# A gated attention and MLP kernel: K, V and Q products of chunks 2 to 8 written as pairs of 64-row halves

## The chip, the cores and the metric

The kernel runs on one NeuronCore of one Trainium2 chip. The metric is the time of one execution on the device, in microseconds (us). Five engines work beside each other, each through its own instruction queue: TensorE (PE for its matmuls, PEld for the weight loads that go with them), VectorE (DVE), ScalarE (ACT), GpSimd (POOL) and SyncE (SP), which here only issues DMAs.

## The reference

Two branches read the same x (2048 tokens of 512 features) and are mixed by a gate per token:

```
qkv = x @ wqkv                                   # 32 heads of 16
pq, pk = q @ w_phi[h], k @ w_phi[h]
phi(p) = concat(softmax(p), softmax(-p))         # per head, 16 + 16 features
kv = sum_s phi_k[s]^T v[s];  z = sum_s phi_k[s]
a  = (phi_q kv / (phi_q z + 1e-6)) @ wo
b  = mish(x @ w1 + b1) @ w2                      # 512 -> 1376 -> 512
g  = sigmoid(sum(x * gate_w))
out = g * a + (1 - g) * b
```

## The kernel before, in words

All large products are taken in fp32r, with each operand split into a high part (h) and the rest (l); a product of two operands is three: h by h, h by l, l by h.

**Stage A** goes over the 2048 tokens in 8 chunks of 256, key ("A", c) with c from 0 to 7; the text counts them as chunks 1 to 8. `w_phi` is multiplied into the K and Q weights first (`fuse`). For each chunk the 512 x features lie as four groups of 128 on the partitions, in two tiles xh and two tiles xl. A chunk has two token tiles of 128, t = 0 and 1. For each of K, V and Q and each tile, `proj` (L230) sends 3 x 4 = 12 products of 128 contraction rows into one PSUM bank (128 tokens x 512 columns): 72 products in a chunk, 6 banks. The steps k0, k1, v0, v1, q0, q1 stand for these groups of 12. All matmuls go through the helper at L101.

What follows K: VectorE takes the maximum and the minimum of each head (mx, mn, L256), the differences (d0, d1, L270 and L272) into a tile E, ACT the exponential, VectorE the sums S (L276), the reciprocal (L284) and the scaled E (ml, L287). GpSimd adds E to zacc (z, L330). V is copied out of PSUM by ACT (ve), Q too (qe), and Q is then stored to DRAM (st). After chunks 3, 6 and 8 TensorE does the `kv` steps of the chunks since the last time: kvp, small products of E and v in 32-column tiles of the array, 32 per chunk, each two records in the profile. In chunks 7 and 8 VectorE also has work of stage B: the softmax of Q's first tiles (out<-pq), the low parts xbl of stage B's x (XL0, XL1, L431) and the sum of zacc.

**Stage B** goes over 4 blocks of 512 tokens. `up` (12 products each, from xbh, w1 and xbl), Mish on ACT, `down` (12 products for four token tiles), `num` (phi_q by kv, in tiles of 64 rows by 32 columns of the array), `wo`. `cd` is four products of 32 contraction rows at four row places, into the four banks of `down`. In the first `up` the products with xbl come last, and they read both halves of it.

**The order** is written out by hand. Strings such as MID, NEXT and LAST (L42 to L58) list the steps; `run` (L201) calls them in turn, and every instruction is pinned, so each engine has its instructions in the order of the string. In stage A the strings put k0 first, then k1, v0, v1, q0, q1, between the steps of other engines. NEXT is chunk 7, LAST chunk 8. Waits between engines are put in from the tiles that they share.

PSUM has eight banks in three rings: "a" with 3, "dn" with 4, "kv" with 1. K and Q go to "a", V of chunks 2 to 8 to "dn".

Of the kernel before, what the change touches and what calls it, by code (L numbers as in the profile page):

```python
# [14 lines left out]
P = 128  # L15
# [4 lines left out]
KT = D // P  # L20
# [19 lines left out]
    S0 rS0 ml0 z0 ldw0 ldw1 S1 rS1 ml1 z1 q0 qe0 st0 q1 qe1 st1  # L40
"""
MID = """  # L42
    k0 xh mx0 mn0 d00 d10 xl ldx k1 wh0 E0 wl0 ldw0 mx1 mn1 d01 d11 v0 wh1 E1 S0 rS0 ml0 z0 ve0 v1 wl1 ldw1
    S1 rS1 ml1 z1 ve1 q0 qe0 st0 q1 qe1 st1
"""
THREE = MID + """ kv" kv' kv """
SIXTH = """
    k0 xh mx0 mn0 d00 d10 xl ldx k1 wh0 E0 wl0 ldw0 mx1 mn1 d01 d11 v0 wh1 E1 S0 rS0 ml0 z0 ve0 v1 wl1 ldw1 lq0+
    S1 rS1 ml1 z1 ve1 q0 qe0 st0 q1 qe1 st1 mx0+ mn0+ kv" kv' kv
"""  # L50
NEXT = """
    lq1+ d00+ d10+ k0 xh mx0 mn0 d00 d10 xl ldx k1 wh0 E0 wl0 ldw0 E0+ mx1 mn1 d01 d11 wh1 E1 S0 rS0 ml0 z0 v0 ve0 wl1 ldw1
    S1 rS1 ml1 z1 v1 ve1 q0 mx1+ mn1+ d01+ d11+ qe0 st0 q1 qe1 st1 E1+
"""
LAST = """
    lq2+ k0 mx0 mn0 d00 d10 k1 ldw0 E0 XH0 mx1 mn1 d01 d11 wx E1 v0 S0 rS0 ml0 z0 ve0 XH1 S1 rS1 ml1 z1 XL0
    v1 ve1 mx2+ mn2+ XL1 q0 qe0 st0 q1 qe1 st1 zt zf zs S0+ zl kv' kv rS0+ km
"""  # L58


# [29 lines left out]
def tile_gated_mix(ctx: ExitStack, tc: tile.TileContext, xT, wv, wkT, wqT, bd, w1a, w1b, b1, w2a, w2b, wo, out):  # L90
    nc = tc.nc
# [5 lines left out]
    pin = tc.keep_in_program_order  # L97
    V, G_, A_, Sy = nc.vector, nc.gpsimd, nc.scalar, nc.sync

    def mm(*a, **k):  # L100
        return pin(nc.tensor.matmul(*a, **k))  # L101

    def T(shape, dt, tag, bufs, name):
        nm[0] += 1
        return sp.tile(shape, dt, name=f"{name}_{nm[0]}", tag=tag, bufs=bufs)

    def k8(name, tag, dt=F32R):
        return T([P, 2048], dt, tag, 2 if tag in ("eT", "E") else 1, name)
# [4 lines left out]
    def k2(name, tag, dt=F32):  # L113
        return T([P, 512], dt, tag, {"pq": 3, "io": 4, "hl": 8}[tag], name)

    def psum(name, tag, bufs={"a": 3, "dn": 4, "kv": 1}):
        nm[0] += 1
        return pp.tile([P, 512], F32, name=f"{name}_{nm[0]}", tag=tag, bufs=bufs[tag])

    def act(out_, in_, fn=AF.Copy, **k):  # L120
        return pin(A_.activation(out_, in_, fn, **k))  # L121

    def kt(t, f):
        return t[:, : KT * f].rearrange("p (k f) -> p k f", f=f)
# [71 lines left out]
    steps = {}  # L196

    def at(key, name, fn):
        steps.setdefault((key, name), []).append(fn)

    def run(text, key, prev=None, nxt=None, prev2=None):  # L201
        for w in text.split():
            k = {"'": prev, '"': prev2, "+": nxt}.get(w[-1], key)
            for fn in steps.pop((k, w.rstrip("'+\"")), ()):
                fn()


    wkh, wkl, wvh, wvl, wqh, wql = [
        kt(k8(n, t), 512) for n, t in (("wkh", "xbh"), ("wkl", "xbl"), ("wvh", "woh"), ("wvl", "wol"), ("wqh", "eT"), ("wql", "eT"))]
    xs, Es, vs, psA, Ep = {}, {}, {}, {}, {}  # L210
# [19 lines left out]
    def proj(x, t, wh, wl, tag, lo_last=False):  # L230
        ps = psum("proj", tag)
        xh, xl = x
        sl = slice(t * P, (t + 1) * P)
        n = 0
        for a, w in ((xh, wh), (xl, wh), (xh, wl)) if lo_last else ((xh, wh), (xh, wl), (xl, wh)):
            for k in range(KT):
                mm(ps, a[k // 2][:, k % 2, sl], w[:, k, :], start=(n == 0), stop=(n == 3 * KT - 1))
                n += 1
        return ps

    def new_x(c):
        xs[c] = [[k2(n, "hl", F32R)[:, :].rearrange("p (k f) -> p k f", f=SC) for _ in range(2)] for n in ("xh", "xl")]
# [7 lines left out]
    def feat_ops(key, t, src, d):  # L250

        n = str(t)

        def red(name, op):
            d[name] = T([P, H], F32, name, 2, name)
            pin(V.tensor_reduce(d[name], hv(src()), axis=AX.X, op=op))  # L256

        def dd(a):
            if "E" not in d:
                pair = key, t // 2  # L260
                if key == ("A", NCH - 1):
                    d["E"] = k4("E", "oh")
                else:
                    if pair not in Ep:
                        e = T([P, NFB * 512], F32, "w2b", 2, "E")[:, :2048] if key in THIRD else k8("E", "E", F32)[:, :]
                        Ep[pair] = e.rearrange("p (t x) -> p t x", t=2)
                    d["E"] = Ep[pair][:, t % 2, :]
            E = hv(d["E"][:, a * 512 : (a + 1) * 512])
            if a == 0:
                pin(V.tensor_sub(E, hv(src()), d["mx"][:, :, None].to_broadcast([P, H, DH])))  # L270
            else:
                pin(V.tensor_sub(E, d["mn"][:, :, None].to_broadcast([P, H, DH]), hv(src())))  # L272

        def ss():
            d["S"] = T([P, 2 * H], F32, "Sm", 2, "Sm")
            pin(V.tensor_reduce(d["S"], hv(d["E"][:, :]), axis=AX.X, op=ALU.add))  # L276

        at(key, "mx" + n, lambda: red("mx", ALU.max))
        at(key, "mn" + n, lambda: red("mn", ALU.min))
        at(key, "d0" + n, lambda: dd(0))  # L280
        at(key, "d1" + n, lambda: dd(1))
        at(key, "E" + n, lambda: act(d["E"], d["E"], AF.Exp))
        at(key, "S" + n, ss)
        at(key, "rS" + n, lambda: pin(V.reciprocal(d["S"], d["S"])))  # L284
# [4 lines left out]
    def a_ops(c):  # L289
        key = ("A", c)  # L290
        P_ = psA[c] = {}
        for t in range(2):
            d = {}
            Es[c, t] = d

            def k_(t=t):
                P_["k", t] = proj(xs[c], t, wkh, wkl, "a")

            def v_(t=t):
                P_["v", t] = proj(xs[c], t, wvh, wvl, "dn" if c else ("kv", "a")[t], lo_last=not c)  # L300

            def q_(t=t):
                P_["q", t] = proj(xs[c], t, wqh, wql, "a")

            def ve(t=t):
                if key in THIRD:
                    if t == 0:
                        Ep[key, "v"] = T([P, NFB * 512], F32, "w2b", 2, "v")
                    vs[c, t] = Ep[key, "v"][:, t * 512 : (t + 1) * 512]
                else:  # L310
                    vs[c, t] = k2("v", "io")
                act(vs[c, t], P_["v", t])

            def qe(t=t):
                P_["qs", t] = k2("qs", "pq")
                act(P_["qs", t], P_["q", t])

            def st(t=t):
                i = 2 * c + t
                pin(Sy.dma_start(pqd[i * P : (i + 1) * P, :], P_["qs", t]))  # L320

            at(key, f"k{t}", k_)
            at(key, f"v{t}", v_)
            at(key, f"q{t}", q_)
            at(key, f"ve{t}", ve)
            at(key, f"qe{t}", qe)
            at(key, f"st{t}", st)
            feat_ops(key, t, lambda t=t: P_["k", t][:, :], d)
            at(key, f"ml{t}", lambda d=d: scale_by(d, V))
            at(key, f"z{t}", lambda d=d: pin(G_.tensor_add(zacc, zacc, d["E"])))  # L330

        def kv():
            if not kvs:
                kvs.append(psum("kvp", "kv")[:, : NG * 64].rearrange("p (g f) -> p g f", g=NG))
            (kvp,) = kvs
            for t in range(2):
                E, v = Es[c, t]["E"], vs[c, t]
                Ev = E[:, :].rearrange("p (a r b x) -> p b r a x", a=2, r=2, b=8)
                for u in range(8):
                    for r in range(2):  # L340
                        o = (u % 2) * 64 + 32 * r
                        mm(kvp[o : o + 32, u // 2, :], v[:, u * 64 + 32 * r : u * 64 + 32 * r + 32], Ev[:, u, r, :, :],
                           start=(c == 0 and t == 0 and u < 2), stop=(c == NCH - 1 and t == 1), skip_group_check=True)

        at(key, "kv", kv)
        if c + 1 < NCH:
            def xh():
                new_x(c + 1)
                for j in range(2):
                    x_hi(c + 1, j)  # L350

            at(key, "xh", xh)
            for j in range(2):
                at(key, "xl", lambda j=j: x_lo(c + 1, j, G_))
        if c + 2 < NCH:
            at(key, "ldx", lambda: ldx(c + 2))
# [455 lines left out]
    for i in range(4):  # L812
        wh, wl = [halves(w, slice(i // 2 * 2, i // 2 * 2 + 2))[i % 2] for w in (wqh, wql)]
# [6 lines left out]

    for t in range(2):
        psA[0]["k", t] = pk[t]
        del steps[("A", 0), f"k{t}"]

    run(FIRST, ("A", 0))
    for c in range(1, NCH):
# [1 line left out]
        run(text, ("A", c), ("A", c - 1), ("B", 0), ("A", c - 2))  # L828
    for b in range(NB):
        run((BLOCK0, BLOCK1, BLOCK, BLOCK)[b], ("B", b), ("B", b - 1), ("B", b + 1))  # L830
    assert not steps, list(steps)


# [58 lines left out]
```

## Time and profile before

| | us |
|---|---|
| median of 3 runs | 444.58 (444.49 to 446.23) |
| span of the profiled execution | 442.5 |
| stage A, from fuse's end to the last kvp's end | 18.7 to 149.35 |
| stage B | 149.35 to 442.5 |

For the profiled execution the page gives its span, from the first to the last instruction, and no other time. Busy times on the page are by engine; the tenths show the busy share of each of 40 equal slices. The chain that ended last is followed back from the last instruction to what released it. In rows of instructions, `E<-E,Sm` is the tile written and the tiles read, L287 the line, `x48` a count, and a last bracket the engine's idle time just before, with what ended it. Matmuls are pipelined, so that a row's length is longer than the distance from one start to the next, and the ends of matmuls are modelled. The whole-array product of 512 columns is shown with 0.39 us and one starts every 0.227 us. The granted TensorE clock is 0.999 of full speed.

### The profile page before, as it was taken

To read this page: it belongs to the slowest core of one execution; us is meant where nothing else is said; L and a number is where in the kernel's file an instruction comes from. 1 tells how busy PE (TensorE), PEld (TensorE's weight loads), DVE (VectorE), ACT (ScalarE), POOL (GpSimd) and SP (SyncE) were. 2 spreads that over 40 slices of the span, in tenths; PEclk is the share of its full clock that TensorE was granted. 3 is DMA by queue.
4 is the path that set the end of the run, shared out by engine and by line. 5 is a ranking of instruction groups with operands and counts; after the bars stand their busy time and mean duration, and the time that the engine had idled before them with its cause. 6 is when DMAs were issued, how large, how long until landed. Compare 5 with 4: busy or idle time off the path is not lost.

```text
span 442.5 us, 7179 instructions
## 1 busy us (share of the span) xinstructions
PE 437.8 (99%) x2874; PEld 359.9 (81%) x2874; DVE 313.2 (71%) x420; ACT 201.4 (46%) x286; POOL 159.6 (36%) x100
## 2 busy tenths in 40 slices
PE   8999999999999999999999999999999999999996
PEld 7888888888888888887888878888878888887885
DVE  3987739559699999999999898279679329601103
ACT  3644523533345455736376533646352645341330
POOL 3078694785662453621024120215310222411121
PEclk9999999999999999999999999999999999999999
DMA  7721631524403136425362533222605302310002
GB/s 265 283 96 48 191 120 50 188 86 133 167 29 116 49 84 209 142 101 168 128 205 96 159 124 120 75 96 95 191 0 192 94 2 96 134 57 1 0 0 96
DMA packets 29001, 49.64 MB, mean 112 GB/s; under 512 B 6308, under 2 KB 15012, under 8 KB 28968
## 3 DMA queue, kind: packets, MB, share of 16 engines
q1 hardware_dynamic: 28648, 48.79, 32.9%
q8 instruction: 22, 0.36, 0.3%
q10 hardware_dynamic: 288, 0.39, 0.3%
q14 instruction: 11, 0.09, 0.1%
q0 software_dynamic: 32, 0.01, 0.0%
HBM read 31.73 MB, written 16.79 MB: 110 GB/s over the span
## 4 chain that ended last, share of the span: by engine, by line
PE 98%; DMA 1%; SPq 0%; DVE 0%; issue 0%
PE proj L101 30%; PE up L101 27%; PE down L101 27%; PE wo L101 10%; PE kvp L101 2%; PE num L101 2%; DMA wT<-in_wkT_dram 1%; PE fuse L101 1%; PE rest L101 0%; DVE io L709 0%; SPq L157 0%; SPq L149 0%
## 5 line engine op out<-in xcount | busy, mean ns | idle before, releaser
L543 POOL TENSOR_TENSOR l<-act,h 128x512 fp32r<-128x512 f32 (+1 forms) x44 | 62.6, 1425 | 215.5 <-ACT h L121 192.7
L121 ACT ACTIVATE act<-up,b1s 128x512 f32<-128x512 f32 x44 | 30.3, 688 | 83.1 <-PE up L101 81.0
L330 POOL TENSOR_TENSOR zacc<-zacc,E 128x1024 f32<-128x1024 f32 x16 | 39.7, 2479 | 39.9 <-DVE E L287 31.4
L121 ACT ACTIVATE E<-E 128x1024 f32<-128x1024 f32 x32 | 33.5, 1060 | 36.0 <-DVE E L272 35.9
L287 DVE TENSOR_TENSOR E<-E,Sm 128x1024 f32<-128x1024 f32 x32 | 45.1, 1409 | 1.0
L101 PE MATMUL wo<-woh,ohl 128*128 128x512 f32 x128 | 41.2, 389 | 0.0
L276 DVE TENSOR_REDUCE Sm<-E 128x64 f32<-128x1024 f32 x32 | 38.5, 1204 | 0.0
L101 PE MATMUL down<-w2ah,h 128*128 128x512 f32 x96 | 37.6, 392 | 0.0
L101 PE MATMUL down<-w2al,h 128*128 128x512 f32 x80 | 31.2, 390 | 0.0
L101 PE MATMUL down<-w2ah,l 128*128 128x512 f32 x80 | 31.1, 389 | 0.0
L121 ACT ACTIVATE h<-act 128x512 fp32r<-128x512 f32 (+2 forms) x48 | 30.3, 632 | 1.6
L101 PE MATMUL down<-w2bh,h 128*128 128x512 f32 x78 | 30.6, 392 | 0.0
L101 PE MATMUL down<-w2bl,h 128*128 128x512 f32 x78 | 30.4, 389 | 0.0
L101 PE MATMUL down<-w2bh,l 128*128 128x512 f32 x78 | 30.4, 389 | 0.0
L431 DVE TENSOR_TENSOR xbl<-xraw,xbh 128x1024 fp32r<-128x1024 f32 x8 | 10.9, 1378 | 27.1 <-ACT xbh L121 27.1
L256 DVE TENSOR_REDUCE mx<-proj 128x32 f32<-128x512 f32 x16 | 11.0, 689 | 25.5 <-PE proj L101 25.5
L101 PEld LDWEIGHTS wo<-woh,ohl 128*128 128x128 f32 x128 | 24.0, 188 | 5.0
L121 ACT ACTIVATE io<-wo,g_sb 128x512 f32<-128x512 f32 x16 | 11.0, 690 | 36.0 <-PE wo L101 34.7
L121 ACT ACT_TABLE_LOAD x19 | 24.4, 1283 | 3.5 <-PE up L101 3.2
L101 PE MATMUL up<-xbh,w1ah 128*128 128x512 f32 x96 | 25.8, 390 | 0.0
L101 PE MATMUL up<-xbh,w1al 128*128 128x512 f32 x96 | 25.7, 389 | 0.0
L101 PE MATMUL up<-xbl,w1ah 128*128 128x512 f32 x96 | 25.7, 389 | 0.0
(125 smaller groups left out, 978.3 us busy)
## 6 DMA issues: line engine op xcount, KB each, us to landing
ed<-E SPq DMA_DIRECT2D x16, 512.0 KB, 2.9
eT<-ed SPq DMA_DIRECT2D x64, 128.0 KB, 3.2
xraw<-in_xT_dram SPq DMA_DIRECT2D x15, 512.0 KB, 4.3
pqd<-qs SPq DMA_DIRECT2D x16, 256.0 KB, 2.1
pq<-pqd SPq DMA_DIRECT2D x16, 256.0 KB, 3.8
out_dram<-io SPq DMA_DIRECT2D x15, 256.0 KB, 2.0
raw<-in_w1a_dram SPq DMA_DIRECT2D x3, 512.0 KB, 4.6
raw<-in_w2a_dram SPq DMA_DIRECT2D x3, 512.0 KB, 3.7
```

Of the source, the lines that this page charges most:

```text
L101: return pin(nc.tensor.matmul(*a, **k))
L121: return pin(A_.activation(out_, in_, fn, **k))
L256: pin(V.tensor_reduce(d[name], hv(src()), axis=AX.X, op=op))
L276: pin(V.tensor_reduce(d["S"], hv(d["E"][:, :]), axis=AX.X, op=ALU.add))
L287: pin(eng.tensor_mul(hv(d["E"][:, :]), hv(d["E"][:, :]), d["S"][:, :, None].to_broadcast([P, 2 * H, DH])))
L330: at(key, f"z{t}", lambda d=d: pin(G_.tensor_add(zacc, zacc, d["E"])))
L431: pin(V.tensor_sub(xb[b][1][:, :, sl], kt(raw[h], SC), f32(xb[b][0][:, :, sl])))
L543: pin(G_.tensor_sub(U[i]["l"][:n, :], U[i]["a"][:n, :], f32(U[i]["h"][:n, :])))
```

## The change

For chunks 2 to 8 the three groups k0, k1 and v0 are sent as one step `(k0|k1|v0)` at the start of the chunk, and v1, q0 and q1 as another, `(v1|q0|q1)`. In each step the 36 products are listed in order and each is written as two products of 64 contraction rows, rows 0 to 63 and rows 64 to 127. The first row half goes through the list from its start, the second from its middle, and they take turns; so at each turn the two halves write to different banks. K stays in the ring "a"; Q of these chunks moves from "a" to "dn". Chunk 1 keeps whole products.

A bank is first written by one half and later by the other. Where the half changes in a bank, the product waits until the last one of the other half in that bank has ended (`hold`). Of a group's 72 half products four have this wait, 56 in all, each for a product 13 to 15 half products before it.

```diff
+    def weave(ops):
+        n = len(ops)
+        todo = [(r, ops[(i + r * (n // 2)) % n]) for i in range(n) for r in (0, 1)]
+        banks = [op[0].name for _, op in todo]
+        last = {b: i for i, b in enumerate(banks)}
+        for i, (r, (out_, a, w, opens, closes)) in enumerate(todo):
+            b, s = banks[i], slice(64 * r, 64 * r + 64)
+            row, ins = newest.get(b, (r, None))
+            if row != r:
+                hold = pin(nc.tensor.nop())
+                tc.add_manual_dep(hold.ins, ins, ...)
+            ins = mm(out_, a[s], w[s], start=opens and banks.index(b) == i, stop=closes and last[b] == i, skip_group_check=True)
+            newest[b] = r, ins.ins.name
...
+    def proj_ops(ps, x, t, wh, wl):
+        xh, xl = x
+        sl = slice(t * P, (t + 1) * P)
+        return [(ps, a[k // 2][:, k % 2, sl], w[:, k, :], True, True) for a, w in ((xh, wh), (xh, wl), (xl, wh)) for k in range(KT)]
...
+            def one(n, wh, wl, tag, t=t):
+                P_[n, t] = psum("proj", tag)
+                return proj_ops(P_[n, t], xs[c], t, wh, wl)
+
+            if c:
+                for n, wh, wl, tag in (("k", wkh, wkl, "a"), ("v", wvh, wvl, "dn"), ("q", wqh, wql, "dn")):
+                    ops[key, f"{n}{t}"] = lambda n=n, wh=wh, wl=wl, tag=tag, one=one: one(n, wh, wl, tag)
...
 MID = """
-    k0 xh mx0 mn0 d00 d10 xl ldx k1 wh0 E0 wl0 ldw0 mx1 mn1 d01 d11 v0 wh1 E1 S0 rS0 ml0 z0 ve0 v1 wl1 ldw1
-    S1 rS1 ml1 z1 ve1 q0 qe0 st0 q1 qe1 st1
+    (k0|k1|v0) xh mx0 mn0 d00 d10 xl ldx wh0 E0 wl0 ldw0 mx1 mn1 d01 d11 wh1 E1 S0 rS0 ml0 z0 ve0 (v1|q0|q1) wl1 ldw1
+    S1 rS1 ml1 z1 ve1 qe0 st0 qe1 st1
 """
```

The strings SIXTH, NEXT and LAST are changed in the same way. `(k0|k1|v0)` stands where k0 stood, and `(v1|q0|q1)` after ve0. The steps of the other engines keep their order.

More of the change, by code (lines that the diff above doesn't have):

```diff
@@ L47 @@
 SIXTH = """
-    k0 xh mx0 mn0 d00 d10 xl ldx k1 wh0 E0 wl0 ldw0 mx1 mn1 d01 d11 v0 wh1 E1 S0 rS0 ml0 z0 ve0 v1 wl1 ldw1 lq0+
-    S1 rS1 ml1 z1 ve1 q0 qe0 st0 q1 qe1 st1 mx0+ mn0+ kv" kv' kv
+    (k0|k1|v0) xh mx0 mn0 d00 d10 xl ldx wh0 E0 wl0 ldw0 mx1 mn1 d01 d11 wh1 E1 S0 rS0 ml0 z0 ve0 (v1|q0|q1) wl1 ldw1 lq0+
+    S1 rS1 ml1 z1 ve1 qe0 st0 qe1 st1 mx0+ mn0+ kv" kv' kv
 """
 NEXT = """
-    lq1+ d00+ d10+ k0 xh mx0 mn0 d00 d10 xl ldx k1 wh0 E0 wl0 ldw0 E0+ mx1 mn1 d01 d11 wh1 E1 S0 rS0 ml0 z0 v0 ve0 wl1 ldw1
-    S1 rS1 ml1 z1 v1 ve1 q0 mx1+ mn1+ d01+ d11+ qe0 st0 q1 qe1 st1 E1+
+    lq1+ d00+ d10+ (k0|k1|v0) xh mx0 mn0 d00 d10 xl ldx wh0 E0 wl0 ldw0 E0+ mx1 mn1 d01 d11 wh1 E1 S0 rS0 ml0 z0 ve0 (v1|q0|q1) wl1 ldw1
+    S1 rS1 ml1 z1 ve1 mx1+ mn1+ d01+ d11+ qe0 st0 qe1 st1 E1+
 """
 LAST = """
-    lq2+ k0 mx0 mn0 d00 d10 k1 ldw0 E0 XH0 mx1 mn1 d01 d11 wx E1 v0 S0 rS0 ml0 z0 ve0 XH1 S1 rS1 ml1 z1 XL0
-    v1 ve1 mx2+ mn2+ XL1 q0 qe0 st0 q1 qe1 st1 zt zf zs S0+ zl kv' kv rS0+ km
+    lq2+ (k0|k1|v0) mx0 mn0 d00 d10 ldw0 E0 XH0 mx1 mn1 d01 d11 wx E1 S0 rS0 ml0 z0 ve0 (v1|q0|q1) XH1 S1 rS1 ml1 z1 XL0
+    ve1 mx2+ mn2+ XL1 qe0 st0 qe1 st1 zt zf zs S0+ zl kv' kv rS0+ km
 """
@@ L101, in mm @@
         return pin(nc.tensor.matmul(*a, **k))
+    def weave(ops):
[8 more added lines that the diff above has]
+                hold = pin(nc.tensor.nop())
+                tc.add_manual_dep(hold.ins, ins, mybir.DependencyInfo(mybir.DependencyClass.Sync, mybir.DependencyReason.DATA), reason="row tiles take turns in a bank")
+            ins = mm(out_, a[s], w[s], start=opens and banks.index(b) == i, stop=closes and last[b] == i, skip_group_check=True)
+            newest[b] = r, ins.ins.name
+    newest = {}
     def T(shape, dt, tag, bufs, name):
@@ L199, in at @@
         steps.setdefault((key, name), []).append(fn)
+    ops = {}
     def run(text, key, prev=None, nxt=None, prev2=None):
         for w in text.split():
+            if w[0] == "(":
+                weave(sum([ops.pop((key, x))() for x in w[1:-1].split("|")], []))
+                continue
             k = {"'": prev, '"': prev2, "+": nxt}.get(w[-1], key)
@@ L294, in a_ops @@
             Es[c, t] = d
-            def k_(t=t):
-                P_["k", t] = proj(xs[c], t, wkh, wkl, "a")
             def v_(t=t):
-                P_["v", t] = proj(xs[c], t, wvh, wvl, "dn" if c else ("kv", "a")[t], lo_last=not c)
+                P_["v", t] = proj(xs[c], t, wvh, wvl, ("kv", "a")[t], lo_last=True)
             def q_(t=t):
@@ L320, in st @@
                 pin(Sy.dma_start(pqd[i * P : (i + 1) * P, :], P_["qs", t]))
-            at(key, f"k{t}", k_)
-            at(key, f"v{t}", v_)
-            at(key, f"q{t}", q_)
+            def one(n, wh, wl, tag, t=t):
[4 more added lines that the diff above has]
+                    ops[key, f"{n}{t}"] = lambda n=n, wh=wh, wl=wl, tag=tag, one=one: one(n, wh, wl, tag)
+            else:
+                at(key, f"v{t}", v_)
+                at(key, f"q{t}", q_)
             at(key, f"ve{t}", ve)
@@ L822, in tile_gated_mix @@
         psA[0]["k", t] = pk[t]
-        del steps[("A", 0), f"k{t}"]
     run(FIRST, ("A", 0))
@@ L830, in tile_gated_mix @@
         run((BLOCK0, BLOCK1, BLOCK, BLOCK)[b], ("B", b), ("B", b - 1), ("B", b + 1))
-    assert not steps, list(steps)
+    assert not steps and not ops, (list(steps), list(ops))
 _OUTS = [((S, D), 'float32')]
```

## The prediction, made before the changed kernel ran

> **What bounds the kernel now.** I read the page first: the busy times, the busy tenths of VectorE (40 slices of 11.06 us each), the chain by line.
>
> ```profile
> PE 437.8 (99%) x2874; PEld 359.9 (81%) x2874; DVE 313.2 (71%) x420; ACT 201.4 (46%) x286; POOL 159.6 (36%) x100
> ...
> DVE  3987739559699999999999898279679329601103
> ...
> PE proj L101 30%; PE up L101 27%; PE down L101 27%; PE wo L101 10%; PE kvp L101 2%; PE num L101 2%; DMA wT<-in_wkT_dram 1%; PE fuse L101 1%; PE rest L101 0%; DVE io L709 0%; SPq L157 0%; SPq L149 0%
> ```
>
> TensorE sets the end: 98% of the chain is its matmuls. VectorE is nearly full too, from slice 10 (110 us), the end of the projections, to about 240 us. The chain in order of time (start, length, what) gives the pace.
>
> ```profile
> 18.72 41.03 PE proj L101 x180
> ...
> 62.56 49.18 PE proj L101 x216
> 111.75 2.82 PE kvp L101 x192
> 114.56 32.86 PE proj L101 x144
> 147.43 1.92 PE kvp L101 x128
> 149.35 11.10 PE up L101 x48
> ...
> 164.99 2.72 PE up L101 x12
> ...
> 437.75 1.44 PE rest L101 x12
> ```
>
> A product of 512 columns takes 2.72/12 = 0.2267 us, one of 256 columns ("rest") 1.44/12 = 0.120. The 256 columns between them cost 0.1067, so 512 columns stream in 0.2133 and each product has a fixed **gap of 0.0133 us**. Re-entering the projections from kvp's quarter-column products costs once 32.86 - 144 x 0.2267 = 0.22. Chunks 7 and 8 are those at 114.56; each chunk has 72 products, 16.32 us. Next, the stretches by engine (PE, PEld, DVE, ACT, POOL busy): an ordinary chunk, chunks 7 and 8, and what follows.
>
> ```profile
> 62.56:78.90 16.34, 16.34 (x73) 13.55 (x73) 11.45 (x14) 4.33 (x6) 9.92 (x7) 1.00 0.30 95
> ...
> 114.56:131.00 16.44, 16.44 (x74) 13.61 (x74) 13.81 (x18) 6.64 (x8) 9.35 (x5) 1.00 0.25 91
> 131.00:147.40 16.40, 16.40 (x77) 13.32 (x78) 16.26 (x17) 7.24 (x9) 6.67 (x4) 1.00 0.29 97
> 147.40:208.00 60.60, 60.60 (x445) 49.63 (x444) 58.46 (x78) 34.65 (x47) 23.93 (x15) 1.00 0.42 133
> ```
>
> An ordinary chunk leaves VectorE 4.9 us idle; chunk 8 leaves 0.1 and the next 60 us leave 2. So a lateness of VectorE that begins in chunk 7 has nothing to be made up in.
>
> **The change, part by part.**
>
> *Concurrency.* 504 whole products become 1008 half ones. Do two halves run at once? The trace has row tiles already: cd, four 32-row products into four banks, and num, 64-row by 32-column ones.
>
> ```profile
> 205.17 0.39 PE L101 MATMUL down<-w2bl,h 128*128 128x512 f32 x1
> 205.40 0.39 PE L101 MATMUL down<-w2bh,l 128*128 128x512 f32 x1
> 205.72 0.51 PE L101 MATMUL down<-w2al,hc 32*128 32x512 f32 x4
> 206.16 0.44 PE L101 MATMUL num<-eT,kvb 64*32 64x256 f32 x7
> ```
>
> The four cd products, each of 128 output columns and 512 streamed ones like the change's, start at 205.72 and num follows at 206.16: 0.44 us for four with their weight loads and two changes of tile shape, where four whole ones take 0.91. They ran together, loads too. I take two halves to run at once.
>
> *Pace of a pair.* Each half still streams 512 columns, so a pair cannot beat 0.2133, and if each half keeps its own gap the pair takes 0.2267 as one product does now. What is the gap? Weight loads (PEld) beside the matmuls:
>
> ```profile
> 256.27 0.39 PE L101 MATMUL down<-w2ah,h 128*128 128x512 f32 x1
> 256.50 0.39 PE L101 MATMUL down<-w2al,h 128*128 128x512 f32 x1
> ```
>
> ```profile
> 256.27 0.19 PEld L101 LDWEIGHTS down<-w2al,h 128*128 128x128 f32 x1
> 256.50 0.19 PEld L101 LDWEIGHTS down<-w2ah,l 128*128 128x128 f32 x1
> ```
>
> The load for the next product starts as the current one starts and is over 0.04 us before the next one begins. So loading is hidden already and two row halves have no exposed load to hide; the gap belongs to the product itself. Bounds: 0.2133 (the other half covers it) and 0.2400 (it is paid for each half in turn). I take 0.2267, nearest to the whole-array row: no gain and no loss on TensorE itself. The Trainium skill, page "TensorE: Matmul & The Clock Gate", section "The mechanism" of Part 3, says a weight load overlaps running matmuls only when the row groups differ; by it the gap would be exposed loading and the halves would remove it. The two rows above, a load wholly beside a matmul of the same rows, speak against it here.
>
> *Entering the 64-row shape.* Once more than before, between chunks 1 and 2: 0.2 by the 0.22 above; the kvp entries remain. The second half starting just behind the first is under 0.01 per group.
>
> *The holds.* Four products per group of 36 wait for the other half's last product in their bank: 56 waits, the awaited one 13 halves (1.5 us) back. Queued behind each is all of TensorE. A wait of TensorE on itself is in the trace already: in the built order the first product of chunk 1's second Q tile has one, at 24.23.
>
> ```profile
> 23.32 1.07 PE L101 MATMUL proj<-wqh,xl 128*128 128x512 f32 x4
> 24.23 1.07 PE L101 MATMUL proj<-wqh,xh 128*128 128x512 f32 x4
> ```
>
> 24.23 - 23.32 = 4 x 0.2267: it cost nothing. I take 0; the upper end is an emptied array each time, 0.39 - 0.23 = 0.16, 9 us in all.
>
> *Q now in the four-buffer ring, V and Q evictions in a burst.* ACT is idle over half of each chunk above, which hides it; SP's stores stand where they stood, the last one's product ends when it did. The x low parts are needed at the third pair instead of the ninth; POOL makes them a chunk ahead.
>
> *When the products finish.* This is what costs. K tile 0 was done after 12 products; woven, its last half is the 60th of 72: it starts 29 x 0.2267 = 6.58 us into the chunk instead of 11 x 0.2267 = 2.49, so **+4.09**. K tile 1 ends with the group: 35 x 0.2267 = 7.94 instead of 5.21, +2.73. VectorE's softmax starts on these tiles (start, length, [idle before]):
>
> ```profile
> 108.11 1.90 DVE L287 TENSOR_TENSOR E<-E,Sm 128x1024 f32<-128x1024 f32 x1
> ...
> 117.55 0.69 DVE L256 TENSOR_REDUCE mx<-proj 128x32 f32<-128x512 f32 x1 [2.25 <-PE proj L101]
> 118.15 0.68 DVE L256 TENSOR_REDUCE mn<-proj 128x32 f32<-128x512 f32 x1
> ...
> 120.27 0.69 DVE L256 TENSOR_REDUCE mx<-proj 128x32 f32<-128x512 f32 x1 [0.24 <-PE proj L101]
> ...
> 132.11 2.88 DVE L272 TENSOR_TENSOR E<-mn,pq 128x512 f32<-128x512 f32 x1
> 134.91 0.68 DVE L256 TENSOR_REDUCE mx<-proj 128x32 f32<-128x512 f32 x1
> ...
> 144.50 1.90 DVE L287 TENSOR_TENSOR E<-E,Sm 128x1024 f32<-128x1024 f32 x1
> ...
> 148.65 2.21 DVE L431 TENSOR_TENSOR xbl<-xraw,xbh 128x1024 fp32r<-128x1024 f32 x1
> ```
>
> In chunks 2 to 6 the 4.9 us of idle time take the lateness. kvp after chunk 6 needs the scaled E of 108.11, done at 110.0, then 114.0; TensorE reaches that E in the last sixth of kvp, 111.75 + 0.2 + 2.35 = 114.3: just in time.
>
> Chunk 7: the first mx moves from 117.55 by 4.09 + 0.2 to 121.84. Four operations at 0.60 follow, so the second mx stands at 124.25 (its tile is there at 123.2): **+4.0** against 120.27. From 120.27 on no idle time is shown before any operation, so all moves by 4.0; chunk 8's first mx would be at 138.9, its tile there by 138.3, so nothing further is added. Then TensorE meets it twice. Chunk 8's kvp needs E of 144.50 + 1.90 = 146.4, then 150.4, and stands there at 147.43 + 0.2 + 1.44 = 149.1: 1.3 us of stall. And up's third part needs the second xbl, 148.65 + 2.21 = 150.86, then 154.86:
>
> ```profile
> 151.22 1.07 PE L101 MATMUL up<-xbl,w1ah 128*128 128x512 f32 x4
> ```
>
> It started at 151.22, 0.36 later; k0's last product of chunk 7 gives the hand-over (116.44 + 3 x 0.227 + 0.39 = 117.51, mx at 117.55: 0.04).
>
> ```profile
> 116.44 1.07 PE L101 MATMUL proj<-wkh,xl 128*128 128x512 f32 x4
> ```
>
> So 0.32 us of slack: TensorE is put back 4.0 - 0.32 = **3.7 us**, the kvp stall within it. After that TensorE has no gap to make it up, and VectorE, late by as much, keeps its place against it.
>
> Sum: 442.5 (span) + 3.7 = 446.2; the runs' median lies 444.58 - 442.5 = 2.1 above the span (start and end around it, since the page gives no other time of this execution), so **448.3 us**.
>
> **The rivals.**
>
> *The gap is hidden by the other half (not slower).* Pair 0.2133. Chunk 7 starts 5 x 72 x 0.0133 - 0.2 = 4.6 earlier, but K tile 0 comes 29 x 0.2133 - 2.49 = 3.7 later in it: first mx -0.9, second -0.9 + 2.42 - 2.72 = -1.2. VectorE then sets the pace to xbl, and TensorE gains 1.2 + 0.3 = 1.5: 443.1. It decides when two starts in one half stand less than 0.226 apart. For it: the bound is not excluded by any row, as no row has two successive 64x128 products. Against: above. The rule of the Trainium skill quoted above is this rival.
>
> *The gap, or the holds, cost time on TensorE.* Pair 0.2400: chunk 7 starts 4.8 + 0.2 = 5.0 later, K tile 0 comes 29 x 0.24 - 2.49 = 4.5 later, mx +9.5, second +9.2, TensorE +8.9: 453.5. Holds at 0.16: 40 of them before chunk 7, 6.4 us, and with the main case's lateness 455.
>
> *The halves do not run at once.* 504 x 0.2267 = 114 us more, VectorE hidden: 559. The cd rows speak against it.
>
> *VectorE makes it up.* E of 132.11 took 2.88 beside POOL's work where others take 0.68; were such meetings with POOL to fall otherwise, up to 3 us return and the time is about 445.5. Against: the POOL work that it meets
>
> ```profile
> 131.59 2.85 POOL L330 TENSOR_TENSOR zacc<-zacc,E 128x1024 f32<-128x1024 f32 x1
> ```
>
> follows VectorE's own scaled E, and moves with it.
>
> **How the numbers follow.** Main case 0.62 (448.3, its own range 446.3 to 449.5); hidden gap 0.14; VectorE makes it up 0.06; gap or holds paid 0.13; one after the other 0.04; rest 0.01. Faster or slower counts beyond 0.5% (2.2 us), about what a measurement of this kernel tells from no change: 442.4 and 446.8. The hidden gap at its full bound stays inside, but 0.04 may pass it; inside are 0.10 of it, most of the fourth rival and some of the main case: 0.18. Slower 0.78. The range goes from 443.6, most of the hidden gap, to 454.
>
> **What would show it.** Products of one half 0.227 apart, two halves' starts close together (right); 0.213 or 0.24 (rivals); halves in turn at 0.113 each are the same pace. The first mx of chunk 7 about 4.3 us later within a chunk of the old length, VectorE without idle time behind it, TensorE idle about 1.3 us in kvp and 2.2 us before up's xbl. I am wrong if stage A's chunks change length, or if VectorE is late and TensorE does not wait there.

## The result, and the profile after

| | before | changed |
|---|---|---|
| median, us | 444.53 (444.28 to 446.23, 4 runs) | 448.66 (448.51 to 448.71, 4 runs) |
| span of the profiled execution, us | 442.5 | 446.9 |

The changed kernel is slower: its runs to those of before have the ratio 1.0088 (95% interval 1.007 to 1.0106). The forecast was 448.3 us.

The page of the changed kernel, the lines that answer to those of before: engines' busy time, VectorE's tenths, and the chain that ended last.

```profile
PE 439.3 (98%) x3378; PEld 360.5 (81%) x3378; DVE 313.8 (70%) x420; ACT 200.5 (45%) x286; POOL 159.8 (36%) x100
...
DVE  3968556577799999999999998359769329601103
...
PE 64%; DVE 3%; issue 0%
```

The matmul records grow by 504 and TensorE's busy time by 1.5 us: half products in pairs take the time of whole ones. VectorE's busy time is nearly the same. What is new stands in the chain: it was 98% TensorE, and now, followed back from the end, it leaves TensorE at up's xbl and runs through VectorE's work of chunk 8, where the profile traces it no further back (so the shares sum to 67%). The view of waits, of TensorE alone, says where (who waited for whom: us in total, times, longest):

```profile
PE up L101 <- DVE xbl L462: 1.7, 1, 1.7
PE kvp L101 <- DVE E L314: 1.4, 1, 1.4
PE warm L101 <- DVE ones L188: 1.1, 1, 1.1
```

The same view of the kernel before:

```profile
PE warm L101 <- DVE ones L171: 1.1, 1, 1.1
PE fuse L101 <- DMA wT<-in_wkT_dram: 0.2, 1, 0.2
```

The waits in up and kvp are new; the third was there before. Now TensorE in order of time, from chunk 1's last whole products on (start, length, what):

```profile
26.60 1.07 PE L101 MATMUL proj<-wqh,xl 128*128 128x512 f32 x4
27.60 0.49 PE L101 MATMUL proj<-wkh,xh 64*128 64x512 f32 x1
27.60 0.49 PE L101 MATMUL proj<-wkl,xh 64*128 64x512 f32 x1
27.93 0.39 PE L101 MATMUL proj<-wkh,xh 64*128 64x512 f32 x1
27.94 0.39 PE L101 MATMUL proj<-wkl,xh 64*128 64x512 f32 x1
...
35.91 0.39 PE L101 MATMUL proj<-wvh,xh 64*128 64x512 f32 x1
35.92 0.39 PE L101 MATMUL proj<-wql,xh 64*128 64x512 f32 x1
...
42.71 0.39 PE L101 MATMUL proj<-wql,xh 64*128 64x512 f32 x1
42.72 0.39 PE L101 MATMUL proj<-wqh,xh 64*128 64x512 f32 x1
...
44.07 0.39 PE L101 MATMUL proj<-wkh,xh 64*128 64x512 f32 x1
44.08 0.39 PE L101 MATMUL proj<-wkl,xh 64*128 64x512 f32 x1
```

The two halves start within 0.01 us of each other, and the six pairs from 42.71 to 44.07 take 1.36/6 = 0.227 us each, the pace of one whole product before. The whole group (v1|q0|q1) of chunk 2, from 35.91 to the next group's start at 44.07, takes 8.16 = 36 x 0.2267. VectorE from the end of chunk 6's share on (a last bracket is its idle time just before, with the releaser):

```profile
112.69 1.91 DVE L314 TENSOR_TENSOR E<-E,Sm 128x1024 f32<-128x1024 f32 x1
...
117.63 1.78 DVE L299 TENSOR_TENSOR E<-mn,pq 128x512 f32<-128x512 f32 x1
122.47 0.69 DVE L283 TENSOR_REDUCE mx<-proj 128x32 f32<-128x512 f32 x1 [3.05 <-PE proj L101]
...
124.86 0.69 DVE L283 TENSOR_REDUCE mx<-proj 128x32 f32<-128x512 f32 x1
...
139.50 0.68 DVE L283 TENSOR_REDUCE mx<-proj 128x32 f32<-128x512 f32 x1
...
149.09 1.89 DVE L314 TENSOR_TENSOR E<-E,Sm 128x1024 f32<-128x1024 f32 x1
...
153.22 2.22 DVE L462 TENSOR_TENSOR xbl<-xraw,xbh 128x1024 fp32r<-128x1024 f32 x1
```

VectorE sits idle for 3.05 us in front of chunk 7's first maximum, and its timeline shows no idle time again up to xbl. And TensorE there:

```profile
148.19 1.55 PE L101 MATMUL kvp<-E,v 128*32 128x64 f32 x96
151.12 0.65 PE L101 MATMUL kvp<-E,v 128*32 128x64 f32 x32 [1.38 <-DVE E L314]
151.70 1.20 PE L101 MATMUL up<-xbh,w1ah 128*128 128x512 f32 x4
152.74 1.08 PE L101 MATMUL up<-xbh,w1al 128*128 128x512 f32 x4
155.49 1.21 PE L101 MATMUL up<-xbl,w1ah 128*128 128x512 f32 x4 [1.68 <-DVE xbl L462]
```

The last quarter of kvp starts at 151.12, when the E of 149.09 + 1.89 = 150.98 is there; the products with xbl start at 155.49, 0.05 after xbl's 153.22 + 2.22 = 155.44.

### The profile page after: what moved, and what is told of

Its sections match the earlier page's. It is cut to its first block, busy times and chain, and to the rows that moved or that the text cites. A ratio compares the mean times of both kernels' runs of the same rounds, so it can differ in the third digit from the quotient of the medians.

```text
span 446.9 us, 8184 instructions
## 1 busy us (share of the span) xinstructions
PE 439.3 (98%) x3378; PEld 360.5 (81%) x3378; DVE 313.8 (70%) x420; ACT 200.5 (45%) x286; POOL 159.8 (36%) x100
## 4 chain that ended last, share of the span: by engine, by line
PE 64%; DVE 3%; issue 0%
PE up L101 26%; PE down L101 26%; PE wo L101 10%; PE num L101 2%; DVE xbl L462 1%; DVE Sm L303 1%; PE rest L101 0%; DVE E L314 0%; DVE mx L283 0%; DVE mn L283 0%; DVE Sm L311 0%; DVE E L297 0%; DVE E L299 0%; DVE io L740 0%
## 5 line engine op out<-in xcount | busy, mean ns | idle before, releaser
L314 DVE TENSOR_TENSOR E<-E,Sm 128x1024 f32<-128x1024 f32 x32 | 46.1, 1440 | 1.0
L101 PE MATMUL proj<-wkl,xh 64*128 64x512 f32 (+1 forms) x120 | 33.9, 390 | 0.0
L101 PE MATMUL proj<-wql,xh 64*128 64x512 f32 (+1 forms) x120 | 33.1, 386 | 0.0
L101 PE MATMUL proj<-wkh,xh 64*128 64x512 f32 (+1 forms) x120 | 32.8, 390 | 0.1
L101 PE MATMUL proj<-wkh,xl 64*128 64x512 f32 (+1 forms) x120 | 32.4, 387 | 0.0
L101 PE MATMUL proj<-wvh,xh 64*128 64x512 f32 (+1 forms) x120 | 32.1, 387 | 0.0
L101 PE MATMUL proj<-wvh,xl 64*128 64x512 f32 (+1 forms) x120 | 32.0, 386 | 0.0
L101 PE MATMUL proj<-wqh,xh 64*128 64x512 f32 (+1 forms) x120 | 32.0, 386 | 0.0
L101 PE MATMUL proj<-wvl,xh 64*128 64x512 f32 (+1 forms) x120 | 32.0, 386 | 0.0
L101 PE MATMUL proj<-wqh,xl 64*128 64x512 f32 (+1 forms) x120 | 32.0, 386 | 0.0
```

The lines of the kernel that those rows point to most:

```text
L314: pin(eng.tensor_mul(hv(d["E"][:, :]), hv(d["E"][:, :]), d["S"][:, :, None].to_broadcast([P, 2 * H, DH])))
```

## The experiments

The theory (lateness): woven halves end K later; VectorE, with no slack in chunks 7 and 8, hands the lateness to TensorE. The rival (TensorE): the half products themselves, their shape and their holds cost the time. Each run's comparison is with runs of the kernel before on the same chip, whose medians were 444.56 (first four) and 444.58 us.

**e1_order_only** has no halves, only the late order (and Q in the ring "dn", as in the changed kernel).

```diff
     def weave(ops):
-        n = len(ops)
-        todo = [(r, ops[(i + r * (n // 2)) % n]) for i in range(n) for r in (0, 1)]
...
+        k0, k1, v0 = ops[:12], ops[12:24], ops[24:]
+        todo = k0[:11] + k1[:11] + v0[:7] + k0[11:] + v0[7:11] + k1[11:] + v0[11:]
...
-            ins = mm(out_, a[s], w[s], ...)
+            mm(out_, a, w, ...)
```

> Products stay whole (128 rows); only their order in a group of 36 is changed, so that K tile 0 ends with the 30th product, K tile 1 with the 35th and V with the 36th, as in the changed kernel. Lateness theory (the time is VectorE's late start on K in chunks 7 and 8): first mx of chunk 7 about 4.1 us later than before, 448.2 us, less than the changed kernel by the one entry into the 64-row shape (0.2 us). TensorE theory (the halves themselves, their shape and holds cost the time): as before, 444.5 us.

Measured: 448.35 us (ratio 1.0078, interval 1.0065 to 1.0092). TensorE's waits in this kernel, which has only whole products in these chunks:

```profile
PE up L101 <- DVE xbl L455: 1.7, 1, 1.7
PE kvp L101 <- DVE E L307: 1.4, 1, 1.4
```

The same two waits, of the same length. Without any halves, 448.35 - 444.56 = 3.8 of the change's 4.1 us are there. That is the lateness theory's number, and not the rival's. The run by itself does not part the order from Q's new ring, though no wait of TensorE on the copies out of a ring is listed; e6_v_first, where the ring and the halves stay and only v0 goes ahead of K, shows what K's place alone does.

**e2_first5** and **e3_last2** split the chunks: halves in chunks 2 to 6 only, and in 7 and 8 only.

```diff
-            if c:
+            if 0 < c < NCH - 2:        # e2_first5;  e3_last2: if c >= NCH - 2
                 for n, wh, wl, tag in (("k", wkh, wkl, "a"), ...):
                     ops[key, f"{n}{t}"] = ...
+            elif c:
+                ...                    # whole products, steps and strings as before
```

> Halves in chunks 2 to 6 only; chunks 7 and 8 whole and in the order of before. Lateness theory: K of chunk 7 comes in time again, but VectorE ends chunk 6's share at about 118.9 instead of 115.3 us, so the first mx of chunk 7 is 1.3 us late instead of 4.3, and TensorE 0.7: 445.3 us (444.8 to 445.6). TensorE theory, in proportion to the halved products (5 of 7 chunks): 447.4 us.

Measured: 445.11 us (1.0014, 1.0005 to 1.0023). The first mx of chunk 7 in e2_first5's timeline of VectorE:

```profile
116.98 1.78 DVE L299 TENSOR_TENSOR E<-mn,pq 128x512 f32<-128x512 f32 x1
118.68 0.68 DVE L283 TENSOR_REDUCE mx<-proj 128x32 f32<-128x512 f32 x1
```

It follows VectorE's own previous work at once and is 118.68 - 117.55 = 1.1 us late against before. The lateness of five chunks is made up in their idle time, but for a rest. The view of waits lists neither E nor xbl for this kernel, but it leaves short waits out, and the rows show one:

```profile
149.44 2.22 DVE L468 TENSOR_TENSOR xbl<-xraw,xbh 128x1024 fp32r<-128x1024 f32 x1
```

```profile
150.50 1.07 PE L101 MATMUL up<-xbh,w1al 128*128 128x512 f32 x4
151.72 1.21 PE L101 MATMUL up<-xbl,w1ah 128*128 128x512 f32 x4
```

xbl ends at 151.66, and the products with it start 0.06 later, as in the changed kernel. At the pace of 0.227 they would have started at 150.50 + 0.91 = 151.41: TensorE waits 0.3 us. They are 151.72 - 151.22 = 0.5 later than before, where 0.7 was expected, and that is the run's loss.

> Halves in chunks 7 and 8 only; chunks 2 to 6 whole and in the order of before. Lateness theory: nearly the whole loss, 448.2 us. TensorE theory, in proportion (2 of 7 chunks): 445.7 us.

Measured: 448.41 us (1.0082, 1.0068 to 1.0096): 3.85 us from 144 of the 504 products, with the two waits of e1_order_only, 1.4 us for E and 1.7 us for xbl. A cost of the halves would be in proportion to their number; this one is not.

**e4_pairs** weaves over two banks, so that K is less late but each hold is near.

```diff
-    (k0|k1|v0) xh mx0 mn0 d00 d10 xl ldx ... ve0 (v1|q0|q1) wl1 ldw1
-    S1 rS1 ml1 z1 ve1 qe0 st0 qe1 st1
+    (k0|k1) xh mx0 mn0 d00 d10 xl ldx ... (v0|v1) wh1 E1 ... ve0 wl1 ldw1
+    S1 rS1 ml1 z1 ve1 (q0|q1) qe0 st0 qe1 st1
```

> Halves woven over two banks, (k0|k1), (v0|v1), (q0|q1): K tile 0 ends 2.7 us later than before instead of 4.1, K tile 1 in time. But both halves change banks at the same turn, so each hold waits for the product just before it instead of one 13 to 15 half products back. Lateness theory with holds that cost nothing: 446.9 us. With holds that empty the array, about 0.3 us once per group of 24, 21 groups of them: chunk 7 starts 4.5 us later and the end is near 451.6 us. TensorE theory without a cost of holds: 448.7 us.

Measured: 453.61 us (1.02, 1.0186 to 1.0213), slower still. TensorE in e4_pairs around a turn of the banks (x8 is four pairs):

```profile
29.38 1.08 PE L101 MATMUL proj<-wkh,xl 64*128 64x512 f32 x8
30.52 1.20 PE L101 MATMUL proj<-wkh,xh 64*128 64x512 f32 x8
31.56 1.08 PE L101 MATMUL proj<-wkl,xh 64*128 64x512 f32 x8
```

Four pairs of 0.227 end at 30.29; the first pair after the holds starts at 30.52, and its four take 1.04 instead of 0.91. So this turn costs 0.23 + 0.13 = 0.36 us. Over nine turns, from the start of kvp after chunk 3 to that after chunk 6, TensorE takes 118.01 - 62.59 = 55.42 us, where it took 111.68 - 59.68 = 52.00 before: 0.38 a turn, where I expected 0.3. 21 turns make 8.0 instead of 6.3, which is 1.7 of the 2.0 us that the forecast missed; the view of waits has another 0.5 us for xbl. The reading of the holds stands: free where the awaited product is 13 to 15 halves back, dear where it is the one just before.

**e5_in_turn** sends first all first halves of a group, then all second ones.

```diff
-        todo = [(r, ops[(i + r * (n // 2)) % n]) for i in range(n) for r in (0, 1)]
+        todo = [(r, ops[i]) for r in (0, 1) for i in range(n)]
```

> The same half products, but in each group of 36 first all of rows 0 to 63 and then all of rows 64 to 127, so that successive products are of the same half. If two halves run side by side only where neighbours in the order are of different halves: one half product every 0.227 us, 114 us more than before, 559 us. If the halves cost the same in any order: 448.7 us.

One run: 540.36 us, beside 444.58. The direction is that of the first reading, but 19 us are missing to 559. TensorE in this kernel where the rows change (wvh,xl are the last of rows 0 to 63, wkh,xh the first of rows 64 to 127):

```profile
33.96 1.07 PE L101 MATMUL proj<-wvl,xh 64*128 64x512 f32 x4
34.87 0.39 PE L101 MATMUL proj<-wvh,xl 64*128 64x512 f32 x1
34.88 0.49 PE L101 MATMUL proj<-wkh,xh 64*128 64x512 f32 x1
35.10 0.39 PE L101 MATMUL proj<-wvh,xl 64*128 64x512 f32 x1
35.21 0.39 PE L101 MATMUL proj<-wkh,xh 64*128 64x512 f32 x1
35.32 0.39 PE L101 MATMUL proj<-wvh,xl 64*128 64x512 f32 x1
35.44 0.39 PE L101 MATMUL proj<-wkh,xh 64*128 64x512 f32 x1
35.55 0.39 PE L101 MATMUL proj<-wvh,xl 64*128 64x512 f32 x1
35.67 0.39 PE L101 MATMUL proj<-wkh,xh 64*128 64x512 f32 x1
35.91 1.08 PE L101 MATMUL proj<-wkl,xh 64*128 64x512 f32 x4
```

Inside one half, products start every 0.227 us (34.87, 35.10, 35.32, 35.55): a half costs as much as a whole. At the change the first product of the other half starts at 34.88, while three products that stand ahead of it in the program have still to start. From there to 35.55 the two halves run side by side. One after the other, the fifth product of the new half would start at 35.55 + 5 x 0.227 = 36.68; it starts at 35.91, 0.77 earlier. There are 14 such changes inside groups and 11 between groups with no kvp between them: the trace shows the same rhythm of starts at all 25, and 25 x 0.77 = 19 us is what was missing.

**e6_v_first** makes K later still.

```diff
-    (k0|k1|v0) xh mx0 mn0 ...
+    (v0|k0|k1) xh mx0 mn0 ...
```

> The changed kernel with (v0|k0|k1) in place of (k0|k1|v0): both K tiles end with the group, K tile 0 another 1.4 us later than in the changed kernel. Lateness theory: chunk 7's softmax another 1.4 us later, and the kvp stages after chunks 3 and 6, which were just in time, now wait about 1.1 us each, so 452.2 us. TensorE theory: as the changed kernel, 448.7 us.

Measured: 452.55 us (1.0191, 1.0162 to 1.022). TensorE's waits in e6_v_first:

```profile
PE kvp L101 <- DVE E L314: 5.0, 3, 2.7
PE up L101 <- DVE xbl L462: 1.7, 1, 1.7
```

All three kvp stages now wait: 2.7 us after chunk 8, and (5.0 - 2.7)/2 = 1.15 each after chunks 3 and 6, where 1.1 was expected. With e1 this is the second point on the same line: later K, later end, with the halves and the rings unchanged.

No run was faster than the kernel before. Halves give TensorE no pace, and the arrangement that loses least, e2_first5, is where K of the last two chunks is whole and in the order of before.

## Why the prediction was right, point by point

**Concurrency: right.** A group of 36 pairs took the time of 36 whole products (8.16 us, rows at 35.91 and 44.07), and e5_in_turn shows the other side: halves of the same rows each cost a whole product's 0.227 us.

**Pace of a pair: right, at the value taken, 0.227.** The gap of 0.013 us stayed with each pair. The Trainium skill's rule on weight loads ("TensorE: Matmul & The Clock Gate", "The mechanism" in Part 3), by which halves would hide it, is not borne out here: neighbours were of different row groups throughout, and the pair's 0.227 is the whole product's.

**Entry: right.** The first two pairs stand at 27.60 and 27.93, 0.33 apart instead of 0.227, and the first is 0.09 late behind the last whole product, which started at 26.60 + 3 x 0.227 = 27.28: 0.2.

**Holds at nothing: right for their distance.** The group from 35.91 to 44.07 has four of them and takes 36 x 0.2267 and no more. The upper end of their price was too low: e4_pairs shows 0.38 us a turn where the awaited product is the one just before, where I bounded it by 0.16.

**K's lateness: right.** The first mx of chunk 7 came 122.47 - 117.55 = 4.9 us later, where 4.3 were worked out. The rest lies ahead of the change: in this execution chunk 1, which is the same in both kernels, already ran 0.56 us later (its second Q tile's last product at 27.28 instead of 26.72). The other executions put that product between 26.62 (e2_first5, whose chunks 1 to 6 are those of the changed kernel) and 27.29 (e3_last2, whose chunks 1 to 6 are those of before), so it is the spread of the start and not the change. The second mx was 124.86 - 120.27 = 4.6 late (4.0 and the 0.56), chunk 8's 139.50 (138.9 and the 0.56). One reading of the tenths was off: slice 10 of VectorE has a 6 and the nines begin with slice 11, at 122 us, and the projections go on to 147.4; the sum, which goes by the rows, does not rest on it.

**The two stalls: right.** TensorE before, at the same places:

```profile
26.04 1.07 PE L101 MATMUL proj<-wqh,xl 128*128 128x512 f32 x4
...
147.36 1.99 PE L101 MATMUL kvp<-E,v 128*32 128x64 f32 x128
149.28 1.20 PE L101 MATMUL up<-xbh,w1ah 128*128 128x512 f32 x4
```

Up's start went from 149.28 to 151.70 (2.4) and xbl's products from 151.22 to 155.49 (4.27). Less the 0.83 that TensorE was behind at kvp's start (148.19 against 147.36: the 0.56 of the start, and the entry), the stalls cost 1.6 and 1.8 us, where 1.3 and 2.2 were expected. Less the 0.56 of the start alone, TensorE is put back 4.27 - 0.56 = 3.7 us at xbl, the term of the sum. After it the lateness stays: 4.4 us at the end of the span.

**The sum.** The span was put at 446.2 and is 446.9, 0.56 of the difference being that start. The time around the span was put at 2.1; the changed kernel's profiled run took 448.68, so it is 1.8. Runs of the kernel before that list both figures show 1.7 as well (444.56 with a span of 442.9): 2.1 came from setting the span of one execution against the median of others. The two misses have opposite signs and cancel in part, which is luck: the forecast of 448.3 is nearer to the median than the span's is to the span.

**VectorE makes it up: did not happen.** The operation that took 2.88 us beside GpSimd's addition took 2.88 again, 4.58 us later (136.69); the addition beside it moved with it, from 131.59 to 136.19.

## What to carry to other kernels

Splitting a product that already fills the contraction rows gained nothing here, though the halves run side by side: each half streams all its 512 columns, and a pair takes the 0.227 us of the whole product, gap included. What changes is when results are complete: interleaving groups makes all of them end near the end of the interleaved stretch, so look for who waits for the first one, and whether that engine has idle time left after it. Before mixing the order, take the stretch in which the consumer is full (here two chunks of eight, in the table by stretch) and price the lateness there.

## What the runs showed of the hardware that was not expected

Matmuls of different row halves did not start in the program's order: in e5_in_turn a product of rows 64 to 127 started at 34.88, ahead of three products of rows 0 to 63 that precede it in the program and started at 35.10, 35.32 and 35.55. The Trainium skill, page "TensorE: Matmul & The Clock Gate", section "The mechanism" of Part 3, says that matmuls start and end in program order; the starts of the trace differ, and the measurement decides (the ends are modelled, so the trace does not settle them). For two halves that share a bank, the program's order is then no safeguard by itself; what happens there without the hold no run shows.

A hold on the product just before cost 0.23 us of waiting and another 0.13 in the four pairs that follow it (e4_pairs), and 0.38 us a turn over nine turns, some 1.7 times a product; holds on a product 13 to 15 halves back cost nothing that the rows show.
